# First chunk's softmax spread before normalizing, with the last down projection in 288-column pieces

## The chip, the cores and the metric

The kernel runs on one core of a Trainium2 chip. The metric is the device time of one execution in microseconds. The engines are TensorE (PE; its weight loads are shown as PEld), VectorE (DVE), ScalarE (ACT), GpSimd (POOL) and SyncE (SP), which here only issues DMAs.

## The reference

Four layers run one after the other on one sequence of 2048 rows of 576 values, all in bf16: attention, gated unit, attention, gated unit, each with a layer norm ahead and a residual sum behind. Both attention layers use the same weights, and so do both gated units.

```python
def _A_ref(x, wqkv, wo):            # H = 32 heads of Dh = 18; W, dil = 8, 2
    q, k, v = split(x @ wqkv)
    idx = pos[:, None] - arange(W)[None, :] * dil      # 8 keys, 2 rows apart, looking back
    logits = einsum("bhsd,bhswd->bhsw", q, k[idx]) * Dh ** -0.5
    logits = where(idx >= 0, logits, -1e9)
    o = einsum("bhsw,bhswd->bhsd", softmax(logits), v[idx])
    return o.reshape(B, S, D) @ wo

def _B_ref(x, w_gate, w_up, w_down):                   # F = 4608
    return ((x @ w_gate) * (x @ w_up)) @ w_down

x = x + _A_ref(_layernorm(x), A_wqkv, A_wo)
x = x + _B_ref(_layernorm(x), B_w_gate, B_w_up, B_w_down)
# the same two lines once more
```

## The kernel before

**Chunks.** The sequence is worked through in chunks of 256 rows; the first 256 rows of the first attention layer are two chunks of 128 rows. Each chunk `j` goes through `attention(j, ...)` and then `glu(j, ...)`. Eight blocks of 128 rows pass the first pair of layers, then the second pair, then the other eight blocks do the same, which makes 17 chunks.

**A planner sets the order.** Every step is an `op` with an engine, a cost in ns, keys that it reads and writes, a priority and a rank. `Plan.run` takes the steps greedily by the earliest time at which they could start by those costs, and emits the instructions in that order; each engine then works in that fixed order. A step of higher rank (a later chunk's attention) is put behind one of lower rank that is already a candidate and would be ready soon, by the tables `GUARD`, `SLACK` and `IDLE`, where `IDLE` is 2000 ns for rank 0. Where the planner sees TensorE idle in the opening, `fill` puts dummy products there (L1091), whose result nobody reads.

**The first chunk** (`j == 0`, called `fast`) runs alone in the opening:

- `head` does the layer norm: `bn_stats` (L414, L418), the inverse root by logarithm and exponential on ScalarE (L429, L430), the shift on VectorE (L434), the apply on ScalarE (L440), TensorE transposes (L456, L458) and one ScalarE copy of the transposed rows (L461).
- `project` makes queries, keys and values (L531); ScalarE and VectorE evacuate them (L613, L615, L642, L649), and ScalarE keeps the last rows for the next chunk (L660). The permuted copies of the weights (L355) are made on VectorE and ScalarE just ahead.
- Keys times queries on VectorE in four products (L686), each summed over the head's dimension by 20 small TensorE products with `Esel` (L701) into one PSUM bank. There the logits stand with head and quarter of the rows on partitions, and 8 offsets x 32 rows along the columns.
- `soft1` clamps the first 14 rows against `cap` on the first 32 partitions (L726), since those keys would lie ahead of the sequence, and takes the maximum (L727). `less` subtracts it (L731), ScalarE takes the exponential (L734), `soft2` the sum (L738), then come the reciprocal (L743) and `soft3`, the product with it (L741), whose result is `a_c`.
- `spread` copies `a_c` to all lanes of each head by TensorE products with `Bsel`, two quarters per PSUM bank (L756); ScalarE copies the first bank to `ab`, VectorE the second (L615, L613). Both use the same bank, one after the other. Of the two `boot` banks the other is held from the start for the result (`bo[1]`).
- `pv` multiplies values by these weights, one product for each of the 8 offsets (L786), in two buffers in turn, and `gather` adds them up in PSUM with an identity product: 512 columns in `bo[0]` (L790) and 128 in `bo[1]` (L791).
- ScalarE evacuates `bo[0]` and VectorE `bo[1]` to `oT` (L803, L805); `wo` is the output projection in two halves of 288 columns (L840); `res` adds the input (L810); and the next `head` follows, whose transposed rows `xnT_B` start the gated unit (L890).

**The gated unit** of a 256-row chunk uses the two halves of the array's rows at once (L914): ScalarE copies the gate (L925), VectorE multiplies it with the other product into `h` (L926). Each of three phases ends with a down projection, `down2`, of 12 blocks of 128 rows of `w_down` for each of two row blocks `i`. A product of 512 columns (L982) and one of 64 (L983) share the block of `h`; `settle2` adds the two parts to the residual on VectorE (L962). The last phase of the last chunk runs alone, with nothing behind it to overlap. Its order is written out by hand:

```python
order = [(1, x) for x in lead] + [(0, x) for x in spans(ph)] + [(1, x) for x in spans(ph)[8:]]
```

so row block 0 ends first, then row block 1. Each block's two settles write bf16 into the residual's own buffer, and one DMA of 128 x 576 on SP's queue stores it.

## Time and profile before

| | us |
|---|---|
| three runs | 1053.73, 1053.96, 1058.55 |
| median | 1053.96 |
| the profiled execution | 1053.36 |
| its span, first to last instruction | 1051.4 |

| engine | busy, us | share of the span |
|---|---|---|
| TensorE products | 1035.9 | 99% |
| TensorE weight loads | 832.5 | 79% |
| VectorE | 782.5 | 74% |
| ScalarE | 410.2 | 39% |
| GpSimd | 8.9 | 1% |

The span is counted in the trace from 0 and all places in this document are microseconds from there. The granted TensorE clock is 1.000. A duration in a row is that of one instruction, or of the stretch from the first to the last where a row stands for several (its last columns say how many). Products overlap: the distance between two starts is less than the duration of one, so both are given where it matters. Dummy products count as busy.

### The profile page before, as it was taken

How to read it: one execution, taken by the hardware profiler on the slowest of the kernel's cores; microseconds unless marked ns; L12 is line 12 of the kernel's file. 1: busy time of each engine (PE TensorE's matmuls, PEld its weight loads, DVE VectorE, ACT ScalarE, POOL GpSimd, SP SyncE). 2: the span in 40 equal slices, each digit the busy share in tenths (PEclk: the TensorE clock that was granted, in tenths of full speed). 3: DMA queues.
4: the chain of work that ended last, by engine and by line, in shares of the span. 5: the costliest groups of instructions: out<-in, count | busy, mean ns of one | idle time of the engine just before them, and what ended most of it. 6: DMA issues, size and time to landing. Idle time of an engine off the chain costs nothing.

```text
span 1051.4 us, 40011 instructions
## 1 busy us (share of the span) xinstructions
PE 1035.9 (99%) x17890; PEld 832.5 (79%) x17901; DVE 782.5 (74%) x1443; ACT 410.2 (39%) x1105; POOL 8.9 (1%) x33
## 2 busy tenths in 40 slices
PE   7999999999999999999999999999999999999998
PEld 4788788789888887778887777877887788777775
DVE  7598987988889879797979573775879748833332
ACT  6743533243434453334434233434344252232221
POOL 3000000000000000000000000000000000000000
PEclk9999999999999999999999999999999999999999
DMA  9957334442536443335352624233352334353432
GB/s 283 340 165 216 88 101 118 137 112 89 100 90 133 137 80 121 107 111 167 86 128 75 179 71 133 95 99 94 94 150 82 103 86 131 113 139 92 124 94 69
DMA packets 144252, 129.66 MB, mean 123 GB/s; under 512 B 43408, under 2 KB 143440, under 8 KB 144080
## 3 DMA queue, kind: packets, MB, share of 16 engines
q1 hardware_dynamic: 144080, 127.10, 42.6%
q8 instruction: 140, 2.29, 0.9%
q14 instruction: 32, 0.26, 0.1%
HBM read 114.02 MB, written 4.19 MB: 112 GB/s over the span
## 4 chain that ended last, share of the span: by engine, by line
PE 83%; DVE 10%; DMA 4%; ACT 1%; SPq 1%; issue 1%; DVEq 0%; ACTq 0%
PE pg L914 17%; PE pu L914 16%; PE pu L982 6%; PE acct L914 6%; PE pa L914 6%; PE pg L982 5%; PE pa L982 5%; PE acct L982 4%; PE pg L531 3%; PE pu L531 3%; DVE scr L786 2%; DVE oT L800 2%; PE pg L819 2%; DMA scr<-a_dram 1%; PE pg L942 1%; PE pu L890 1%
## 5 line engine op out<-in xcount | busy, mean ns | idle before, releaser
L914 PEld LDWEIGHTS <-wg 64*128 64x128 bf16 x4320 | 393.7, 94 | 30.8 <-issue 2.9
L914 PE MATMUL pg<-xnT_B,wg 64*128 64x256 bf16 x3200 | 412.3, 269 | 1.6 <-ACT xnT_B L461 1.1
L914 PEld LDWEIGHTS <-wu 64*128 64x128 bf16 x4320 | 392.4, 94 | 25.3 <-issue 1.7
L914 PE MATMUL pu<-xnT_B,wu 64*128 64x256 bf16 x3200 | 411.3, 269 | 1.0 <-DVE h L926 0.9
L982 PEld LDWEIGHTS <-h 64*128 64x128 bf16 x2136 | 129.1, 94 | 101.0 <-DVE h L926 0.7
L983 PE MATMUL pu<-wd,h 64*128 64x64 bf16 (+1 forms) x1020 | 192.8, 189 | 0.1
L983 PE MATMUL pg<-wd,h 64*128 64x64 bf16 (+1 forms) x1020 | 192.8, 189 | 0.0
L926 DVE TENSOR_TENSOR h<-pu,g_sb 128x512 bf16<-128x512 f32 x218 | 147.1, 686 | 49.6 <-ACT g_sb L925 48.6
L925 ACT CAST g_sb<-pg 128x512 bf16<-128x512 f32 x218 | 126.9, 586 | 105.0 <-PE pg L914 86.5
L475 ACT COPY tok<-pu 1x1 f32<-1x1 f32 x291 | 42.7, 147 | 318.9 <-PE pu L914 213.2
L914 PE MATMUL acct<-xnT_B,wg 64*128 64x256 bf16 x1120 | 152.8, 269 | 0.0
L914 PE MATMUL pa<-xnT_B,wu 64*128 64x256 bf16 x1120 | 152.4, 269 | 0.2
L982 PE MATMUL pu<-wd,h 64*128 64x512 bf16 x576 | 149.3, 377 | 0.3 <-ACT tok L475 0.3
L982 PE MATMUL pg<-wd,h 64*128 64x512 bf16 x576 | 149.1, 377 | 0.0
L983 PEld LDWEIGHTS <-h 64*128 64x128 bf16 x2136 | 127.9, 95 | 1.6 <-issue 1.1
L982 PE MATMUL pa<-wd,h 64*128 64x512 bf16 (+1 forms) x491 | 127.0, 377 | 0.0
L982 PE MATMUL acct<-wd,h 64*128 64x512 bf16 (+1 forms) x492 | 126.8, 377 | 0.0
L531 PEld LDWEIGHTS <-wqkv 64*128 64x128 bf16 (+1 forms) x2030 | 103.6, 94 | 14.5 <-issue 2.6
L707 DVE TENSOR_TENSOR scr<-qT,kv 128x1280 bf16<-128x1280 bf16 x112 | 88.5, 816 | 25.7 <-ACT kv L615 25.7
L914 PE MATMUL pg<-xnT_B,wgu_t 64*128 64x256 bf16 x400 | 107.6, 269 | 0.0
L914 PE MATMUL pu<-xnT_B,wgu_t 64*128 64x256 bf16 x400 | 107.6, 269 | 0.0
L531 PE MATMUL pg<-xnT_A,wqkv 64*128 64x256 bf16 (+2 forms) x863 | 100.5, 265 | 0.2 <-ACT wqkv L355 0.2
(156 smaller groups left out, 1488.7 us busy)
## 6 DMA issues: line engine op xcount, KB each, us to landing
wd<-in_B_w_down_dram SPq DMA_DIRECT2D x306, 288.0 KB, 4.6
scr<-a_dram SPq DMA_DIRECT2D x56, 128.0 KB, 2.7
wg<-in_B_w_gate_dram SPq DMA_DIRECT2D x6, 768.0 KB, 9.2
wu<-in_B_w_up_dram SPq DMA_DIRECT2D x6, 768.0 KB, 10.8
out_dram<-xf SPq DMA_DIRECT2D x16, 144.0 KB, 2.9
xb<-in_A_x_dram SPq DMA_DIRECT2D x7, 288.0 KB, 2.9
a_dram<-scr SPq DMA_DIRECT2D x14, 128.0 KB, 2.3
scr<-in_A_wqkv_dram SPq DMA_DIRECT2D x4, 288.0 KB, 3.5
```

Of the source, the lines that this page charges most:

```text
L475: box["at"] = nc.scalar.copy(tok[0:1, :], src())
L531: return nc.tensor.matmul(bank(p_, u)[0:m, e * n:(e + 1) * n], lhsT=wqkv[r_, k, w0:w0 + m], rhs=xnT_A[r_, k, c0:c0 + n], start=start, stop ...
L707: op("DVE", 70 + 2.6 * n, lambda p_=p_, e=e: nc.vector.tensor_tensor(late["prod"][p_ % 2][:, e, :, 0:n], qT[:, :, 0:n], kT[:, :, HALO - DI ...
L786: nc.vector.tensor_tensor(js(dst), js(vT[:, :, o0:o0 + n]), abw, op=ALU.mult)
L800: op("DVE", 70 + 2.63 * n, lambda i_=i_: nc.vector.tensor_tensor(oT[:, :, 0:n], oT[:, :, 0:n], late["prod"][i_ % 2][:, 0, :, 0:n], op=ALU. ...
L819: return nc.tensor.matmul(bank(hh, us[i])[:, 0:HD], lhsT=oT[rows, t, i * P:(i + 1) * P], rhs=wo_p[rows, t, hh * HD:(hh + 1) * HD], start=( ...
L890: nc.tensor.matmul(pt[:, e * n:(e + 1) * n], lhsT=w_[:, k, ft * P:(ft + 1) * P], rhs=xT[:, k, 0:n], start=(first and k == 0 and e == 0), s ...
L914: return nc.tensor.matmul(ps[:, e * n:(e + 1) * n], lhsT=w_, rhs=xT[rows, k, 0:n], start=(first and e == 0 and k == 0), stop=(not first an ...
L925: op("ACT", 490, lambda: nc.scalar.copy(g_sb[gs][:, 0:ul], pg[use["slot"]][:, 0:ul]), r=[f"wg_{j}_{u}"], w=[f"g{gs}"], prio=0, due=True)
L926: op("DVE", 605, lambda: nc.vector.tensor_tensor(hb[hs][:, 0:ul], pu[use["slot"]][:, 0:ul], g_sb[gs][:, 0:ul], op=ALU.mult), r=[f"wu_{j}_{ ...
L982: return [lambda: nc.tensor.matmul((pg, pu)[i][use["slot"]][:], lhsT=lhs, rhs=wt[rows, e % 2, 0:512], start=first, stop=fin, skip_group_ch ...
L983: lambda: nc.tensor.matmul((pg, pu)[i][tl["slot"]][:, 0:TL], lhsT=lhs, rhs=wt[rows, e % 2, 512:D], start=first, stop=fin, skip_group_check ...
```

## The change

The first chunk's exponentials are written as bf16 straight into `a_c` and are spread unnormalized. Sum and reciprocal run beside that; the reciprocal is split into two bf16 parts (`rz`), which eight TensorE products with `Bsel` (`sums`) spread and add up in columns 128 to 255 of `bo[1]`; ScalarE copies them to `rzs`, and the evacuation of the gathered values becomes three VectorE products with `rzs`. The output projection is cut into three steps, each of which waits for its own part of `oT`.

The mask is added instead of clamped: `cap` is now zero except for -1e9 at the masked places, and one TensorE product with the identity adds it to the logits bank of each layer's first chunk, behind the first group of logits.

The first chunk's second layer norm splits its apply, and the copy of the transposed rows, between ScalarE and VectorE. In the last down projection each product has 288 columns, half of a row; the four quarters (row block, half) end one after the other, with a settle of 128 x 288 for each into a buffer of its own (`outb`) and a DMA of its own.

```diff
     Bsel = sb("Bsel", [P, 4, 4, 32])
-    cap = sb("cap", [32, W, HALO], FP32)
+    cap = sb("cap", [P, W, HALO])
+    rz = sb("rz", [P, 2, P // 4])
+    rzs = sb("rzs", [P, P], FP32)
...
     wd = [sb(f"wd{i}", [P, 2, D]) for i in range(NWD)]
+    outb = xb[0]
...
         def mk_cap():
-            nc.gpsimd.memset(cap[:], 3e38)
+            nc.gpsimd.memset(cap[:], 0.0)
...
                 if wlist[i_] > 0:
-                    nc.gpsimd.memset(cap[:, i_, 0:DIL * wlist[i_]], -1e9)
+                    nc.gpsimd.memset(cap[0:32, i_, 0:DIL * wlist[i_]], -1e9)
...
                     nc.scalar.activation(y[:, D:D + TL], x[:, KF * P:D], ACT.Identity, **sc)
-            if "n" in parts:
+            two = halves and nst == 1
+            if two:
+                op("ACT", 490, lambda i=i: nc.scalar.activation(xn[ia + i][:, 0:320], src(i)[:, 0:320], ACT.Identity,
+                                                                bias=nmr[:, ia + i:ia + i + 1], scale=rstd[:, ia + i:ia + i + 1]),
+                   r=[keys[i], nk[i], rk[i]], w=[f"xn{ab}{ia + i}"], prio=prio)
+                op("DVE", 330, lambda i=i: nc.vector.tensor_scalar(xn[ia + i][:, 320:D], src(i)[:, 320:D], rstd[:, ia + i:ia + i + 1],
+                                                                   nmr[:, ia + i:ia + i + 1], op0=ALU.mult, op1=ALU.add),
+                   r=[keys[i], nk[i], rk[i]], w=[f"xn{ab}{ia + i}h"], prio=prio)
+            elif "n" in parts:
...
                     nc.tensor.transpose(bf(b())[r_:r_ + TL, KF, :], xn[ia + i][:, KF * P:D], ident[:])
-            o = op("PE", 290, tr, r=[f"xn{ab}{ia + i}", "ident"], prio=0, margin=mg, **b.take())
+            o = op("PE", 290, tr, r=[f"xn{ab}{ia + i}", "ident"] + [f"xn{ab}{ia + i}h"] * two, prio=0, margin=mg, **b.take())
             pl.also(o, [key + str(ia + i)])
+            if two:
+                b.use["left"] = 2
+                op("ACT", 420, lambda i=i, b=b, cs=cs: nc.scalar.copy(dst[:, 0:3, cs], bf(b())[:, 0:3]), r=[b.key], w=[key + str(ia + i)],
+                   prio=prio, **b.drop())
+                op("DVE", 330, lambda i=i, b=b, cs=cs: nc.vector.tensor_copy(dst[:, 3:KT, cs], bf(b())[:, 3:KT]), r=[b.key], w=[key + str(ia + i) + "h"],
+                   prio=prio, **b.drop())
+                continue
...
                                          stop=(i_ == len(srcs()) - 1), skip_group_check=True)
+                if t0 == 0 and p_ == 0:
+                    nc.tensor.matmul(pav[0:32, :, 0:HALO], lhsT=ident[:, 0:32], rhs=cap[:], start=False, stop=True, skip_group_check=True)
...
                 op("PE", 20 * 20, lambda p_=p_: esel(p_, lambda: [late["prod"][p_ % 2][:, :, k, :] for k in range(KT)]),
-                   r=["sel", pk], prio=0, **kw)
+                   r=["sel", pk, "cap", "ident"], prio=0, **kw)
...
             op("PE", 250 + 4 * max(45, 0.215 * n), lambda: [esel(p_, lambda p_=p_: [late["s1"][p_]]) for p_ in range(W // 2)],
-               r=["sel", "s10", "s11", "s12", "s13"], prio=0, margin=mg, **b1.take())
+               r=["sel", "s10", "s11", "s12", "s13", "cap", "ident"], prio=0, margin=mg, **b1.take())
...
             pav = wv(b1())
-            if t0 == 0:
-                nc.vector.tensor_tensor(pav[0:32, :, 0:HALO], pav[0:32, :, 0:HALO], cap[:], op=ALU.min)
...
             nc.vector.tensor_tensor(wv(late["Lt"]), pav, mx_t[:, 0:sq].unsqueeze(1).to_broadcast([P, W, sq]), op=ALU.subtract)
-        op("DVE", 130 + 2.1 * n + (250 if t0 == 0 else 0), soft1, r=[b1.key] + (["cap"] if t0 == 0 else []), w=["mx"], prio=prio - 1)
+        op("DVE", 130 + 2.1 * n, soft1, r=[b1.key], w=["mx"], prio=prio - 1)
         op("DVE", 130 + 2.1 * n, less, r=[b1.key, "mx"], w=["Lt"], prio=prio - 1, **b1.drop())
-        op("ACT", 109 + 1.66 * n, lambda: nc.scalar.activation(late["Lt"][:, 0:W * sq], late["Lt"][:, 0:W * sq], ACT.Exp),
-           r=["Lt"], w=["Lt"], prio=prio - 1)
+        ex = "a_c" if fast else "Lt"
+        op("ACT", 109 + 1.66 * n, lambda: nc.scalar.activation(late[ex][:, 0:W * sq], late["Lt"][:, 0:W * sq], ACT.Exp),
+           r=["Lt"], w=["s13" if fast else "Lt"], prio=prio - 1)
...
         def soft2():
-            nc.vector.tensor_reduce(out=zs_t[:, 0:sq], in_=wv(late["Lt"]).rearrange("p w s -> p s w"), op=ALU.add, axis=AX.X)
+            nc.vector.tensor_reduce(out=zs_t[:, 0:sq], in_=wv(late[ex]).rearrange("p w s -> p s w"), op=ALU.add, axis=AX.X)
...
             nc.vector.tensor_tensor(wv(late["a_c"]), wv(late["Lt"]), zs_t[:, 0:sq].unsqueeze(1).to_broadcast([P, W, sq]), op=ALU.mult)
-        op("DVE", 140 + 3.5 * n, soft2, r=["Lt"], w=["z"], prio=prio - 1)
+        op("DVE", 140 + 3.5 * n, soft2, r=["s13" if fast else "Lt"], w=["z"], prio=prio - 1)
         op("DVE", 300 + n, lambda: nc.vector.reciprocal(zs_t[:, 0:sq], zs_t[:, 0:sq]), r=["z"], w=["zs"], prio=prio - 1)
-        op("DVE", 86 + 2.05 * n, soft3, r=["Lt", "zs"], w=["s13"], prio=prio - 1)
+        if fast:
+            def parts_of():
+                nc.vector.tensor_copy(rz[:, 0], zs_t[:, 0:sq])
+                nc.vector.tensor_tensor(rz[:, 1], zs_t[:, 0:sq], rz[:, 0], op=ALU.subtract)
+            op("DVE", 180, parts_of, r=["zs"], w=["rz"], prio=prio - 1)
+        else:
+            op("DVE", 86 + 2.05 * n, soft3, r=["Lt", "zs"], w=["s13"], prio=prio - 1)
...
                     op("PE", 330, gather, r=["prod0", "ident"], w=[bo[0].key, bo[1].key], prio=0, hold=bo[0].pool, use=bo[0].use)
+
+                    def sums():
+                        for e in range(2):
+                            for jj in range(4):
+                                nc.tensor.matmul(bo[1]()[:, n + sq * jj:n + sq * (jj + 1)], lhsT=Bsel[:, jj].rearrange("p a b -> p (a b)"), rhs=rz[:, e],
+                                                 start=False, stop=(e == 1), skip_group_check=True)
+                    op("PE", 480, sums, r=["rz", "sel", bo[1].key], w=["rzp"], prio=0.5)
+                    op("ACT", 230, lambda: nc.scalar.copy(rzs[:], bo[1]()[:, n:2 * n]), r=["rzp"], w=["rzs"], prio=0)
...
         if fast:
-            op("ACT", 490, lambda: nc.scalar.copy(oT[:, 0:KF, 0:n], bo[0]()[:, 0:KF * n].rearrange("p (k s) -> p k s", k=KF)),
-               r=[bo[0].key], w=["oT"], prio=0, **bo[0].drop())
-            op("DVE", 200, lambda: nc.vector.tensor_copy(oT[:, KF, 0:n], bo[1]()[:, 0:n]), r=[bo[1].key], w=["oTt"], prio=0, **bo[1].drop())
+            bo[0].use["left"] = 2
+            for m in range(2):
+                op("DVE", 400, lambda m=m: nc.vector.tensor_tensor(oT[:, 2 * m:2 * m + 2, 0:n], bo[0]()[:, 2 * m * n:2 * (m + 1) * n].rearrange("p (k s) -> p k s", k=2),
+                                                                   rzs[:].unsqueeze(1).to_broadcast([P, 2, n]), op=ALU.mult),
+                   r=[bo[0].key, "rzs"], w=["oTm" if m else "oT"], prio=0, **bo[0].drop())
+            op("DVE", 200, lambda: nc.vector.tensor_tensor(oT[:, KF, 0:n], bo[1]()[:, 0:n], rzs[:], op=ALU.mult), r=[bo[1].key, "rzs"], w=["oTt"], prio=0, **bo[1].drop())
...
-                def wo(i=i, hh=hh, b=b):
-                    for t in range(KT):
+                def wo(ts, i=i, hh=hh, b=b):
+                    for t in ts:
...
-                o = op("PE", 620, wo, r=["oT", "oTt", *wok], prio=0, margin=mg, **b.take())
+                o = None
+                for ts, ky in (((0, 1), "oT"), ((2, 3), "oTm"), ((4,), "oTt")) if fast else ((range(KT), "oT"),):
+                    kw = b.take() if o is None else dict(w=[b.key], after=o)
+                    o = op("PE", 124 * len(ts), lambda ts=ts, wo=wo: wo(ts), r=[ky, *wok] + ["oTt"] * (not fast), prio=0, margin=mg, **kw)
...
         fk = [f"xf{(t0 // 2) % NXS}_{i0 + i}" for i in range(nst)]
-        xT, xk = xnT_B[j % NXB], [f"xB{j % NXB}_{i}" for i in range(nst)]
+        xT, xk = xnT_B[j % NXB], [f"xB{j % NXB}_{i}" for i in range(nst)] + ["xB0_0h"] * (j == 0)
...
                 return second
-            todo = {0: spans(ph), 1: spans(ph)}
-            lead = spans(ph)[:8]
-            order = [(1, x) for x in lead] + [(0, x) for x in spans(ph)] + [(1, x) for x in spans(ph)[8:]]
-            for x, (i, (m, e, ft)) in enumerate(order):
+            lead, rest = spans(ph)[:8], spans(ph)[8:]
+            pts = [(0, 0), (0, 1), (1, 0), (1, 1)]
+            order = [(p_, x) for p_ in pts[:3] for x in lead] + [(p_, x) for p_ in pts[:3] for x in rest] + [(pts[3], x) for x in lead + rest]
+            for x, ((i, hh), (m, e, ft)) in enumerate(order):
                 kw = dict(pair=(use, tl)) if x == 0 else {}
-                bb("PE", 122, lambda i=i, m=m, e=e, ft=ft: [f() for f in two(i, slice(0, P), m, e, ft, ft == n0, ft == n1)],
-                   r=[f"h{hsl[m]}", f"wd{wb(ft)}"], w=[f"acc{j}_{ph}{i}"], **kw)
+
+                def part(i=i, hh=hh, m=m, e=e, ft=ft):
+                    nc.tensor.matmul((pg, pu)[i][(use, tl)[hh]["slot"]][:, 0:HD], lhsT=hb[hsl[m]][:, e * n + i * P:e * n + (i + 1) * P],
+                                     rhs=wd[wb(ft)][:, e % 2, hh * HD:(hh + 1) * HD], start=ft == n0, stop=ft == n1, skip_group_check=True)
+                bb("PE", 122, part, r=[f"h{hsl[m]}", f"wd{wb(ft)}"], w=[f"acc{j}_{ph}{i}{hh}"], **kw)
                 if ft == n1:
-                    settle2(i, use, tl, True, f"acc{j}_{ph}{i}")
+                    u = (use, tl)[hh]
+                    cs = slice(hh * HD, (hh + 1) * HD)
+                    at = outb[:, i, cs]
+                    op("DVE", 370, lambda i=i, u=u, cs=cs, at=at: nc.vector.tensor_tensor(at, (pg, pu)[i][u["slot"]][:, 0:HD], xs_f[:, i0 + i, cs], op=ALU.add),
+                       r=[f"acc{j}_{ph}{i}{hh}", fk[i]], w=[f"ob{i}{hh}"], prio=0, free="unit", use=u)
+                    op("SP", 600, dma(ov[:, t0 + i, cs], at), r=[f"ob{i}{hh}"], nbytes=P * HD * 2, prio=2)
```

## The prediction

> **What bounds the kernel now.** I read the page's busy table first, then the busy time by stretches, then the order of time at both ends.
>
> ```profile
> PE 1035.9 (99%) x17890; PEld 832.5 (79%) x17901; DVE 782.5 (74%) x1443; ACT 410.2 (39%) x1105; POOL 8.9 (1%) x33
> ```
>
> TensorE is busy 99% of the span, so between the ends only less TensorE work or fewer waits can help. The stretches (microseconds, PE, PEld, DVE, ACT, POOL busy, clock, DMA) say where it is not:
>
> ```profile
> 20.00:26.00 6.00, 4.72 (x24) 2.16 (x23) 5.04 (x13) 2.14 (x6) 0.00 (x0) 1.00 1.08 328
> 34.00:60.00 26.00, 25.71 (x441) 21.72 (x441) 18.81 (x42) 15.96 (x38) 0.00 (x0) 1.00 1.05 327
> 300.00:350.00 50.00, 48.52 (x858) 42.47 (x854) 45.79 (x91) 24.28 (x67) 0.00 (x0) 1.00 0.42 99
> 600.00:1041.00 441.00, 440.99 (x7798) 350.55 (x7793) 269.02 (x485) 150.45 (x423) 0.00 (x0) 1.00 0.37 108
> ```
>
> Before 34 us TensorE waits for the first chunk and fills with dummy products (L1091), which count as busy. From 34 to 1041 us it idles 4.6 us in all (1007.0 less 1002.4 busy), most of it between 100 and 600 us, where VectorE is busy near 90%. After 1047 us only the last settles and the store remain. So the change can pay at the two ends; a microsecond of the first chunk saved moves everything behind it, as long as TensorE stays fed. The first chunk, in order of time (start, duration, engine, line):
>
> ```profile
> 16.63 0.27 DVE L726 TENSOR_TENSOR pu<-pu,cap 32x112 f32<-32x112 f32 x1
> 17.40 0.42 DVE L731 TENSOR_TENSOR scr<-pu,mx 128x256 f32<-128x256 f32 x1
> 17.92 0.42 ACT L734 ACTIVATE scr<-scr 128x256 f32<-128x256 f32 x1 [0.85 <-DVE scr L731]
> 19.37 0.42 DVE L741 TENSOR_TENSOR scr<-scr,zs 128x256 bf16<-128x256 f32 x1
> 19.85 0.38 PE L756 MATMUL pu<-scr,Bsel 128*128 128x256 bf16 x2 [0.44 <-DVE scr L741]
> 20.26 0.59 ACT L615 CAST scr<-pu 128x512 bf16<-128x512 f32 x1
> 21.37 0.69 DVE L613 CAST scr<-pu 128x512 bf16<-128x512 f32 x1 [0.53 <-DMA wgu_t<-in_B_w_up_dram]
> 22.09 3.94 DVE L786 TENSOR_TENSOR scr<-kv,scr 128x640 bf16<-128x640 bf16 x8
> 26.50 0.59 ACT L803 CAST oT<-pu 128x512 bf16<-128x512 f32 x1 [4.26 <-PE pu L790]
> 27.14 0.79 PE L840 MATMUL pg<-wo_p,oT 128*128 128x288 bf16 x5
> 27.96 0.46 DVE L810 TENSOR_TENSOR xf<-pg,xb 128x288 f32<-128x288 f32 x1
> 31.00 0.87 ACT L440 ACTIVATE xn<-xf,nmr,rstd 128x576 bf16<-128x576 f32 x1 [0.42 <-DVE nmr L434]
> 31.92 0.40 PE L456 MATMUL pg<-ident,xn 128*128 128x128 bf16 x4 [0.49 <-ACT xn L440]
> ```
>
> Each step starts within 0.1 us of the end of the one above or of an unshown one between, so this is a chain. (The wait named as a DMA at L613 is the second spread product, 20.90 to 21.28.) The other end:
>
> ```profile
> 1046.45 0.69 DVE L962 TENSOR_TENSOR xf<-acct,xf 128x512 bf16<-128x512 f32 x1 [3.66 <-PE pg L983]
> 1047.25 0.23 DVE L962 TENSOR_TENSOR xf<-pg,xf 128x64 bf16<-128x64 f32 x1
> 1047.43 0.69 DVE L962 TENSOR_TENSOR xf<-pa,xf 128x512 bf16<-128x512 f32 x1
> 1048.22 0.23 DVE L962 TENSOR_TENSOR xf<-pu,xf 128x64 bf16<-128x64 f32 x1
> ```
>
> TensorE's last product (L983, 1047.23 and 0.19) ends at 1047.42, yet VectorE ends at 1048.45.
>
> **The first chunk, step by step.** (1) The clamp L726 goes: from 16.63 to 16.94, 0.31 us. In its place one product of 112 columns adds the mask. It stands behind the first logits group, and TensorE waits 0.4 us and more for each next group, so it is hidden; uncovered it would be at most 0.22 (the 128-column gather tail L791). The mask is now filled on all partitions by POOL, before at 8.98 to 9.80 and needed at 13.48: cover 3.7 us.
>
> (2) The spread no longer waits for sum, reciprocal and product. From the exponential's end (18.34) to the spread (19.85) was 1.51; a direct hand-over is 0.06 (L741's end to L756), so 1.45 is saved and the spread starts at 19.85 - 0.31 - 1.45 = 18.09. The exponential moves to 17.61; ScalarE's permutation copy ahead of it ends at 17.06, so that holds. Sum (0.58), reciprocal (0.35) and the two small parts (0.25, between the 0.11 and 0.16 of L434 each) run on VectorE from 18.05 to about 19.35; the second spread copy needs VectorE at 19.61. Cover 0.26.
>
> (3) Spread to first value product was 2.24 (19.85 to 22.09), and its terms stay: 0.38 product, 0.59 copy, 0.38 product through the same bank, 0.69 copy, and hand-overs. But ScalarE also has the value evacuations (0.26 and 0.59) and the halo copy (0.31) near there; before, they came first. If they still do, up to 1.16 is added, and not below zero, since the terms cannot shrink. I take 0, because the first spread is ready at 18.47, before the value tails can leave TensorE, and the planner prefers a rank-0 operation due within 2 us. L786 then starts at 20.33.
>
> (4) Eight 32-column products (sums) go between the first gather and the second. At 0.055 each (16 products of L531 at 128 columns take 0.9) that is 0.44. The value products use two buffers in turn, and an even one already waits 0.2 for its gather (period 1.01 for two). The odd ones now do as well: second gather 0.3 later, and this stays to the last. The sums wait for the reciprocal's parts, ready at 19.35, long before the first gather ends at about 21.2; behind them in TensorE's queue stand the gathers alone. Bounds: 0 (sums placed later) to 0.7 (0.10 each, the weight-load row, 0.8 in all). I take +0.30. ScalarE then copies the sums (0.26) out of the bank that the gathers still fill; if the next gather must wait for that copy, 0.27 more, inside these bounds. [...] The traces here show no such pair yet.
>
> (5) The evacuation before the output projection was 0.68 (26.46 to 27.14), ScalarE beside VectorE. Now two VectorE products of 128x256 (0.42 each by L731, 0.46 from start to start) must both end before the bank is free for the projection: 0.04 + 0.46 + 0.42 + 0.04 = 0.96. The third (0.29 by L805) hides behind four projection products at 0.124. So +0.28, from 0.2 (pitch 0.41, as L786's) to 0.5 (third not hidden). The layer-norm statistics of a later chunk that stood at 26.76 to 27.82 lose their slot; they go to VectorE's 3.8 us idle before 34.77.
>
> (6) The apply splits 576 columns into 320 on ScalarE and 256 on VectorE. ScalarE's 0.87 falls by 0.22 (slope from 0.26 at 128 columns to 0.59 at 512) to 0.39 (in proportion); I take 0.30. TensorE idles 0.49 for it now. [...] The transposed copy's split (0.69) saves nothing: TensorE has the next chunk's projection until 33.8.
>
> Start: 1.76 - 0.30 - 0.28 + 0.30 = 1.48 us sooner. Weights allow it: the second weight slice lands by 28.3.
>
> **The tail.** 24 pairs of 512 and 64 columns become 48 products of 288: the same columns. The pairs run at 0.245, L840's 288-column products at 0.124, so 5.9 us either way. The order finishes three quarters early; after the last product one 128x288 settle remains (0.46, L810) in place of 0.69 and 0.23 behind a queue: 1047.42 + 0.03 + 0.46 = 1047.91 against 1048.45, 0.54 saved. The store is 72 KB, not 144 (1.8 us to landing): 0 to 0.25 less at the 330 GB/s of that burst; I take 0.10. Four stores on SP's queue (0.4 each) instead of two, three of them over 1 us earlier. Together 0.64.
>
> **The rest.** The second layer's first chunk pays the mask product on a full TensorE: 0.05 (0 to 0.22); VectorE's 0.27 there is not on the path. The planner orders everything anew; I put 0 on it, between -4.6 (all waits gone) and +4.6 (doubled).
>
> Sum: 1.48 + 0.64 - 0.05 = 2.07. The profiled run took 1053.36 (span 1051.4 and 1.96 around it), giving 1051.3; the median of the runs shown is 1053.96, 0.6 above it, so I forecast 1051.9.
>
> **Rivals.** *ScalarE's queue is next.* Value evacuations stay ahead of the first spread copy (+0.85) and sums cost 0.57: the start gives 0.36, the total 0.95, time 1053.0. For it: their order before. Against: readiness at 18.47. *The start is absorbed.* VectorE's displaced statistics delay the layer norm of the third chunk; its transposes have about 3 us in hand before the projection at 40.68. Only the tail stays: 1053.4. *Slower: VectorE's order from 100 to 600 us.* VectorE is near 90% busy and TensorE already waited 1.1, 0.9 and 0.5 there for single VectorE or ScalarE results. If a new order puts an evacuation of the gated units behind a long attention product, each such place costs 0.5 to 1.1; from three places on the gain is gone, and a doubling (+4.6) gives 1056.5. Against: the shift is nearly uniform. *Better:* the new order loses those waits: down to 1047.3.
>
> **Numbers.** 0.5% is 5.3 us, about what a measurement of this kernel can tell from no change. Forecast 0.45, ScalarE 0.22, absorbed 0.13, slower 0.11, better 0.09. All of the first three lie within 0.5%; of the slower and the better case about 0.07 each pass it, which needs seven or more lost waits, or all waits gone and more at the ends. So 0.07, 0.86, 0.07. The range, 1048.8 to 1055.6, takes in the first three with their bounds and the near halves of the other two.
>
> **What would show it.** L786's successor starts near 20.3; the gathers' period is near 1.01 with one 0.3 slip; the output projection is about 1.2 earlier, the first transposes of the gated stage near 30.4; one settle of about 0.46 ends the kernel, its end 0.5 after the last product. TensorE's idle time from 34 to 1041 us stays near 4.6. A start of the value products past 21, or idle time changed by over 2 us, would make me wrong.

## The result and the profile after

The changed kernel takes 1051.39 us (median of 22 runs, 1049.02 to 1055.67), the kernel before on the same chip 1053.53 (22 runs, 1050.99 to 1058.55). The ratio is 0.9979 with a 95% interval of 0.997 to 0.9987: some 2.2 us less, well within 0.5%. Ratios leave out two runs that were far slower than the rest, one of the kernel before (1076.78) beside the last experiments and one of x_clamp1 (3990.57). The profiled execution took 1051.13 us with a span of 1049.35 (before 1053.36 and 1051.37).

The busy line of the page, and the four stretches that were shown of before (us, then PE, PEld, DVE, ACT, POOL busy, clock, DMA share, GB/s):

```profile
PE 1033.9 (99%) x17898; PEld 827.8 (79%) x17909; DVE 783.3 (75%) x1446; ACT 409.6 (39%) x1105; POOL 8.5 (1%) x33
```

```profile
20.00:26.00 6.00, 4.78 (x34) 2.32 (x34) 4.73 (x12) 2.56 (x8) 0.00 (x0) 1.00 1.08 325
34.00:60.00 26.00, 25.70 (x442) 21.61 (x442) 19.58 (x44) 15.94 (x37) 0.00 (x0) 1.00 1.08 320
300.00:350.00 50.00, 49.43 (x874) 43.37 (x871) 45.98 (x92) 24.34 (x69) 0.00 (x0) 1.00 0.39 99
600.00:1041.00 441.00, 440.99 (x7787) 350.53 (x7784) 268.82 (x483) 151.12 (x423) 0.00 (x0) 1.00 0.37 107
```

TensorE is the bound as before. Its idle time from the first product of the gated unit to the last product is 4.73 us against 4.68, so the middle is unchanged in sum. The opening in order of time (line numbers are those of the changed kernel; L753 is the exponential, L781 the spread, L811 the value products, L826 the sums, L838 the evacuation, L417 the statistics and L443 the apply of later blocks, L437 the shift, L876 the output projection, L846 the residual, L448 the apply, L467 and L469 the transposes, L929 the gated unit):

```profile
17.61 0.42 ACT L753 ACTIVATE scr<-scr 128x256 bf16<-128x256 f32 x1 [0.57 <-DVE scr L749]
18.08 0.38 PE L781 MATMUL pu<-scr,Bsel 128*128 128x256 bf16 x2 [0.76 <-ACT scr L753]
18.55 0.59 ACT L633 CAST scr<-pu 128x512 bf16<-128x512 f32 x1 [0.33 <-PE pu L781]
19.16 0.26 ACT L633 CAST kv<-pu 64x128 bf16<-64x128 f32 x1
...
19.66 0.69 DVE L631 CAST scr<-pu 128x512 bf16<-128x512 f32 x1 [0.19 <-PE pu L781]
20.44 1.51 DVE L811 TENSOR_TENSOR scr<-kv,scr 128x640 bf16<-128x640 bf16 x3
20.98 0.38 PE L815 MATMUL pu<-scr,ident 128*128 128x512 bf16 x1 [0.56 <-DVE scr L811]
21.25 0.35 PE L826 MATMUL pg<-rz,Bsel 128*128 128x32 bf16 x8
21.46 0.38 PE L815 MATMUL pu<-scr,ident 128*128 128x512 bf16 x1
21.86 0.15 DVE L437 SCALAR_TENSOR_TENSOR nmr<-mv,rstd 128x1 f32<-128x1 f32 x1
21.92 0.27 ACT L829 COPY rzs<-pg 128x128 f32<-128x128 f32 x1 [0.92 <-PE pg L816]
...
24.54 0.38 PE L815 MATMUL pu<-scr,ident 128*128 128x512 bf16 x1
25.43 0.76 DVE L838 TENSOR_TENSOR oT<-pu,rzs 128x256 bf16<-128x256 f32 x2 [0.94 <-PE pa L469]
26.24 0.77 PE L876 MATMUL pu<-wo_p,oT 128*128 128x288 bf16 x5 [0.33 <-DVE oT L838]
26.31 0.81 DVE L417 BATCH_NORM_STATS2 st<-xb 128x6 f32<-128x288 bf16 x2
27.27 0.40 DVE L846 TENSOR_TENSOR xf<-pu,xb 128x288 f32<-128x288 f32 x1
...
29.21 0.81 DVE L417 BATCH_NORM_STATS2 st<-xf 128x6 f32<-128x288 bf16 x2
29.74 0.85 ACT L443 ACTIVATE xn<-xb,nmr,rstd 128x576 bf16<-128x576 bf16 x1
30.18 0.11 DVE L437 SCALAR_TENSOR_TENSOR nmr<-mv,rstd 128x1 f32<-128x1 f32 x1
30.49 0.64 ACT L448 ACTIVATE xn<-xf,nmr,rstd 128x320 bf16<-128x320 f32 x1
31.19 0.40 PE L467 MATMUL pu<-ident,xn 128*128 128x128 bf16 x4 [0.45 <-ACT xn L448]
31.80 0.48 ACT L474 COPY xnT_B<-pu 128x384 bf16<-128x384 bf16 x1 [0.67 <-PE pu L469]
32.31 0.29 DVE L476 COPY xnT_B<-pu 128x256 bf16<-128x256 bf16 x1 [0.61 <-ACT xnT_B L474]
```

Exponential (first row) and spread (second row) are now next to each other; in between stood sum, reciprocal and product. From the end of the last 512-column gather (L815, 24.54 + 0.38 = 24.92; its 128-column companion ends at 24.98) to L838 there is a gap that the chain of before had not. And the statistics L417 at 26.31 stand between the evacuation and the residual on VectorE. The end of the kernel:

```profile
1043.80 0.46 DVE L1058 TENSOR_TENSOR xb<-acct,xf 128x288 bf16<-128x288 f32 x1 [2.22 <-PE acct L1051]
...
1046.25 0.46 DVE L1058 TENSOR_TENSOR xb<-pu,xf 128x288 bf16<-128x288 f32 x1 [1.01 <-PE pu L1051]
```

One settle of 0.46 follows TensorE's last product (1046.21), where two and the end of a third followed before.

Since single profiles differ by a shift of the whole opening (up to 0.9 us, of a cause that was not shown; the first statistics, which wait for the first transfer, start at 2.99 in the profile of before and at 2.89 in that of after) and by waits in the middle, the experiments are read by distances inside one run. In us; a gather ends with its 512-column product, which the evacuation reads; "glu" is the first product of the gated unit:

| kernel | exponential to spread | spread to first value product | to end of last gather | to evacuation | to projection | to residual | to glu |
|---|---|---|---|---|---|---|---|
| before | 1.93 | 2.24 | 4.37 | 0.04 | 0.64 | 0.82 | 5.87 |
| after | 0.47 | 2.36 | 4.48 | 0.51 | 0.81 | 1.03 | 5.60 |
| e1_tail | 1.94 | 2.24 | 4.37 | 0.04 | 0.64 | 0.82 | 5.86 |
| e2_open | 0.47 | 2.36 | 4.48 | 0.51 | 0.81 | 1.03 | 5.60 |
| e3_norm | 1.98 | 2.50 | 4.45 | 0.04 | 0.64 | 0.82 | 5.88 |
| e4_clamp | 0.47 | 2.36 | 4.48 | 0.11 | 0.81 | 1.03 | 5.59 |
| e5_whole | 0.47 | 2.36 | 4.48 | 0.51 | 0.81 | 1.03 | 5.81 |
| e6_early_tr | 0.74 | 2.62 | 4.88 | 0.52 | 0.81 | 1.03 | 5.23 |
| e8_stats | 0.93 | 2.36 | 4.48 | 0.52 | 0.81 | 0.81 | 5.40 |
| e9_two_stores | 0.47 | 2.36 | 4.48 | 0.52 | 0.81 | 1.03 | 5.60 |
| e10_onecopy | 0.62 | 2.61 | 4.48 | 0.53 | 0.81 | 1.03 | 5.59 |
| e11_tiny | 0.47 | 2.36 | 4.48 | 0.11 | 0.82 | 1.03 | 5.59 |
| e13_clamp | 0.46 | 2.36 | 4.50 | 0.10 | 0.81 | 1.03 | 5.60 |
| x_clamp1 | 0.47 | 2.35 | 4.50 | 0.11 | 0.81 | 1.03 | 5.60 |

In e3, e6, e8 and e10 the records show a stretch of 3.4 us at half clock between 15 and 19 us (granted 0.50 from 16 to 18 us in each of the four, 1.00 in the changed kernel); that the odd figures of their first two columns (0.62 to 0.93, 2.50 to 2.62) come of it and not of the edits is the author's reading, and no run parts the two.

### The profile page after: what moved, and what is told of

It reads as the page before. It is cut to its first block, busy times and chain, and to the rows that moved or that the text cites. A ratio compares the mean times of both kernels' runs of the same rounds, so it can differ in the third digit from the quotient of the medians.

```text
span 1049.3 us, 40035 instructions
## 1 busy us (share of the span) xinstructions
PE 1033.9 (99%) x17898; PEld 827.8 (79%) x17909; DVE 783.3 (75%) x1446; ACT 409.6 (39%) x1105; POOL 8.5 (1%) x33
## 4 chain that ended last, share of the span: by engine, by line
PE 84%; DVE 10%; DMA 3%; issue 1%; ACT 1%; SPq 1%; DVEq 0%; ACTq 0%
PE pg L953 16%; PE pu L953 16%; PE pu L1021 6%; PE acct L953 6%; PE pa L953 6%; PE pa L1021 5%; PE pg L1021 5%; PE acct L1021 4%; PE pg L549 3%; PE pu L549 3%; DVE scr L811 2%; PE pg L855 2%; DVE oT L833 2%; PE pu L929 2%; PE pg L929 1%; DMA scr<-a_dram 1%
## 5 line engine op out<-in xcount | busy, mean ns | idle before, releaser
L1021 PEld LDWEIGHTS <-h 64*128 64x128 bf16 x2112 | 122.6, 94 | 102.5 <-DVE h L965 1.0
L1022 PE MATMUL pg<-wd,h 64*128 64x64 bf16 x1008 | 190.5, 189 | 0.0
L1022 PE MATMUL pu<-wd,h 64*128 64x64 bf16 x1008 | 190.5, 189 | 0.0
L1021 PE MATMUL pa<-wd,h 64*128 64x512 bf16 x480 | 123.8, 377 | 0.0
L1021 PE MATMUL acct<-wd,h 64*128 64x512 bf16 x480 | 123.7, 377 | 0.0
L1022 PEld LDWEIGHTS <-h 64*128 64x128 bf16 x2112 | 121.6, 95 | 1.2 <-issue 0.4
L549 PEld LDWEIGHTS <-wqkv 64*128 64x128 bf16 (+1 forms) x2030 | 102.8, 94 | 15.8 <-issue 3.5
L549 PE MATMUL pg<-xnT_A,wqkv 64*128 64x256 bf16 (+2 forms) x863 | 100.0, 265 | 1.1 <-DVE xf L1001 0.8
```

The lines of the kernel that those rows point to most:

```text
L549: return nc.tensor.matmul(bank(p_, u)[0:m, e * n:(e + 1) * n], lhsT=wqkv[r_, k, w0:w0 + m], rhs=xnT_A[r_, k, c0:c0 + n], start=start, stop ...
L1021: return [lambda: nc.tensor.matmul((pg, pu)[i][use["slot"]][:], lhsT=lhs, rhs=wt[rows, e % 2, 0:512], start=first, stop=fin, skip_group_ch ...
L1022: lambda: nc.tensor.matmul((pg, pu)[i][tl["slot"]][:, 0:TL], lhsT=lhs, rhs=wt[rows, e % 2, 512:D], start=first, stop=fin, skip_group_check ...
```

## The experiments

**The two ends apart.** e1_tail is the kernel before with the new last down projection (the edit shown), e2_open the changed kernel with the old one (the reverse).

```diff
-            order = [(1, x) for x in lead] + [(0, x) for x in spans(ph)] + [(1, x) for x in spans(ph)[8:]]
+            order = [(p_, x) for p_ in pts[:3] for x in lead] + [(p_, x) for p_ in pts[:3] for x in rest] + [(pts[3], x) for x in lead + rest]
...
```

> The kernel before with the new last down projection alone. Theory (the two ends add up): first value product 22.1, first gated product 33.8, last product 1047.4 as before; last settle ends 0.50 behind it (before 1.03), the store is done 2.6 behind that (before 2.9), span 1050.5. Rival (a new order of the whole moved TensorE's waits): the last product moves by 1 or more although nothing ahead of it was edited.

> The changed kernel with the old last down projection. Theory (the ends add up): first value product 20.4, first gated product 32.9, last product 1046.2, last settle 1.03 behind it, span 1050.2. Rival (order): last product away from 1046.2 by 1 or more.

Times: 1051.97 and 1057.65, one run each, beside 1052.24 of the kernel before. In e2 the last product ends at 1051.58 instead of 1046.2, by the expectation the sign of its rival. But the order of the instructions on VectorE and ScalarE is that of the changed kernel up to the last settles, so a new order is not the cause, and the time of e2 is not to be read as the opening's price: from glu to the last product it lost 5.6 us more than the changed kernel, 1.96 of it as idle time of TensorE in the unaltered middle, and a stretch of 3.4 us at half clock stands near 146 us. The rest of the loss is not explained. The distances are clean. With the old opening e1 has the opening of before to 0.01, with the new one e2 that of after. From the last product's end to the last settle's end: 0.50 in e1 and after, 1.03 in e2 and before. From there to the end of the span: 2.72 and 2.64 with the new tail, 2.92 and 3.18 with the old. The two parts do not act on each other, and the tail is worth 0.53 by the settle and 0.2 to 0.5 by the store.

**Normalizing before the spread again.** e3_norm is the changed kernel with `soft3` ahead of the spread, no sums, and the old evacuation; mask product, split apply and tail stay.

```diff
-        ex = "a_c" if fast else "Lt"
+        ex = "Lt"
...
+        op("DVE", 86 + 2.05 * n, soft3, r=["Lt", "zs"], w=["s13"], prio=prio - 1)
...
-                    op("PE", 480, sums, r=["rz", "sel", bo[1].key], w=["rzp"], prio=0.5)
-                    op("ACT", 230, lambda: nc.scalar.copy(rzs[:], bo[1]()[:, n:2 * n]), r=["rzp"], w=["rzs"], prio=0)
```

> The changed kernel with the first chunk's softmax normalized before the spread, as before, and the old plain evacuation; mask product, split layer norm and new tail stay. Theory (steps add up): first value product 21.8 (0.31 from the mask alone), first gated product 33.3, that is the spread is worth 1.35 at the value products but only 0.4 to 0.5 at the gated unit, since evacuation and displaced statistics give the rest back. Rival (the spread's saving arrives whole): first gated product 34.2.

```profile
18.24 0.42 ACT L753 ACTIVATE scr<-scr 128x256 f32<-128x256 f32 x1 [0.77 <-DVE scr L749]
...
20.22 0.38 PE L775 MATMUL pu<-scr,Bsel 128*128 128x256 bf16 x2
```

Exponential to spread is 1.98 again, against 0.47 in the changed kernel, where the exponentials are spread unnormalized and the granted clock was 1.00 in this stage. The last gather ends 4.45 behind the first value product; there are no sums in that run, but a shift (L437, 0.15) came ahead of the last value product on VectorE. Without either, before and e1 have 4.37. The changed kernel has that shift among its value products too (21.86). But its second gather starts 0.48 behind the first (20.98, 21.46), where it was 0.40 before, and ends with its 128-column product at 21.89; the fourth value product waits for that end and starts at 21.93, so that the shift need not have cost anything there. So the sums cost 0.11 at most. ScalarE's evacuation starts 0.04 behind the gather, as before.

The expected places were missed: the first value product came at 22.72 (21.8) and the first gated product at 34.55 (33.3, the rival 34.2). A later opening (0.57) and the stretch at half clock are in both. At the gated unit there is also another order on TensorE: from the first transposes to glu 2.13 us pass instead of 1.68, because 20 products of the next block's projection stand between instead of 12. So what the spread alone is worth at the gated unit, e3 does not show.

**Why the evacuation starts late.** VectorE's L838 starts 0.51 behind the last gather in the changed kernel; in the kernel before ScalarE's L803 started 0.04 behind its gather. The row names the next block's transposes (L469), which share TensorE. e6_early_tr puts these transposes between the gathers (first lines); e4_clamp has VectorE's clamp back in place of the mask product (last lines).

```diff
+            was, pl.rank = pl.rank, 0 if first_tr else pl.rank
...
+            pl.rank = was
...
+            if t0 == 0:
+                nc.vector.tensor_tensor(pav[0:32, :, 0:HALO], pav[0:32, :, 0:HALO], cap[:], op=ALU.min)
```

> The changed kernel with the second chunk's transposes (L467, L469) put between the gathers instead of behind the last one. Theory A (VectorE's evacuation waited for these transposes, as the wait view says): first evacuation product starts 0.05 behind the end of the last wide gather, 25.0 instead of 25.43, and the output projection at 25.8 instead of 26.24. Theory B (a delay of VectorE's own at this instruction): still 0.5 behind the gather, 25.4. Under both some of the second chunk's projection fills TensorE ahead of the output projection; first gated product 32.3 under A, 32.6 under B.

> The changed kernel with the clamp on VectorE in place of the mask product. Theory: maximum 0.31 later, first value product 20.75, first gated product 33.2. Rival (VectorE had slack there): first value product 20.45 and no change behind.

```profile
25.16 0.38 PE L817 MATMUL pu<-scr,ident 128*128 128x512 bf16 x1
...
26.05 0.76 DVE L840 TENSOR_TENSOR oT<-pu,rzs 128x256 bf16<-128x256 f32 x2 [0.94 <-PE pg L818]
```

This is e6 (its line numbers here are two higher). No transpose stands behind the gather, and the gap is still 0.52 (25.53 to 26.05): the transposes are not what VectorE waits for, and the name in the row was wrong. (The first gated product came at 33.12, later than either theory had it: the gathers took 0.40 longer, and TensorE waited 0.57 for the transposed copy.) In e4, where only the softmax's start was touched, the gap was 0.11. That had not been expected: the evacuation and all that it waits for were the same, and VectorE had one instruction more ahead of it. So the last runs asked what of the clamp does it. e11_tiny keeps the mask product and puts a memset of 32x8, which nobody reads, where the clamp was; e13_clamp is e4 once more, in twelve runs.

```diff
+            if t0 == 0:
+                nc.vector.memset(tiny[:], 0.0)
             nc.vector.tensor_reduce(out=mx_t[:, 0:sq], in_=pav.rearrange("p w s -> p s w"), op=ALU.max, axis=AX.X)
```

> The changed kernel with one more small VectorE instruction (a memset of 32x8) ahead of the maximum, so that every later VectorE instruction stands one place further back, as with the clamp; mask still added on TensorE, nothing else altered. Stream theory (the start of L838 0.51 us behind the last gather is tied to where VectorE's instruction stands in its stream): gap of 0.1 us or less between last gather and first evacuation product, and the output projection 0.9 us behind the gather instead of 1.3. Clamp theory (the gap goes only with what the clamp itself does, a read and write of the score bank on VectorE): the gap stays at 0.51. Chance theory (the gap comes and goes from run to run): either; then the kernel with the clamp, run again beside it, may show 0.5 as well. Time 1050 to 1053 us.

> The kernel with VectorE's clamp in place of the mask product, again, timed. If the 0.11 us gap ahead of the evacuation is a property of the program and not of one run, it is 0.11 again. Forecast from it: 0.4 us sooner at the evacuation, 0.25 to 0.31 later at the maximum, so 0 to 0.2 us sooner at the first gated product than the changed kernel: 1051.2 us, 0.998 of the time before, not to be told from the changed kernel.

```profile
16.76 0.06 DVE L747 MEMSET tiny<- 32x4 uint32 x1
...
24.72 0.38 PE L818 MATMUL pu<-scr,ident 128*128 128x512 bf16 x1
...
25.20 0.76 DVE L841 TENSOR_TENSOR oT<-pu,rzs 128x256 bf16<-128x256 f32 x2 [0.54 <-PE pg L819]
...
26.02 0.77 PE L879 MATMUL pu<-wo_p,oT 128*128 128x288 bf16 x5
```

This is e11 (line numbers three higher). The memset of 0.06 us, eight microseconds earlier, takes 0.40 us out of the evacuation's start: 0.11 behind the gather. All four kernels with one more instruction there have 0.10 or 0.11, all seven others with this evacuation 0.51 to 0.53. So it is neither the clamp nor chance, and not the transposes either, which stand behind the gather in e11 as in the changed kernel. It goes with one more instruction in VectorE's stream. But each of the four edits also changes a buffer that is declared ahead of `rzs` (`cap` in 32 bits, or `tiny`), so that later buffers may lie elsewhere; no run parts the one from the other. What in the engine does it, these runs do not show. Measured from the end of the statistics ahead of the maximum to glu, the changed kernel takes 16.21 (16.66 to 32.87), e13 16.12 (16.47 to 32.59), e11 15.82 (16.82 to 32.64): the clamp costs its 0.31 and saves 0.40 by accident, the memset saves the 0.40 alone.

As times: e13 has 1050.24 (12 runs), a ratio of 0.9967 (0.995 to 0.9984) to the kernel before on its chip; e11 1049.99 in its one run. Neither can be told from the changed kernel.

**The splits of the second layer norm.** e5_whole has apply and transposed copy whole again; e10_onecopy the copy alone, by leaving out the second `if two:` block.

```diff
-            two = halves and nst == 1
+            two = False
```

> The changed kernel with the first chunk's second layer norm whole on ScalarE: one apply, one copy of the transposed rows. Theory (the apply's split saves 0.23, the copy's split costs 0.1 since its halves run one after the other): transposes 31.4 against 31.19, their copy 0.69 long and done by about 32.7 against 32.60, first gated product 33.0 against 32.87. Rival (both splits save): first gated product 33.3 or later.

> The changed kernel with the transposed copy of the first chunk's second normalization whole again on ScalarE (the apply stays split). Bank theory (the two halves read one PSUM bank and ran one after the other, 0.80 us in all against 0.69 for the whole copy): first gated product 0.1 us sooner from the transposes on, transposes to first gated product 1.55 to 1.6 instead of 1.68. Rival (the split copy helps as planned): 0.15 us later. Time within 0.3 us of the changed kernel, 0.998 of before.

```profile
31.30 0.40 PE L467 MATMUL pu<-ident,xn 128*128 128x128 bf16 x4 [0.45 <-ACT xn L448]
...
31.91 0.69 ACT L472 COPY xnT_B<-pu 128x640 bf16<-128x640 bf16 x1 [0.67 <-PE pu L469]
...
32.98 0.62 PE L922 MATMUL pg<-xnT_B,wg 128*128 128x128 bf16 x8
```

Residual to glu is 5.81 with both whole, 5.59 with the copy whole, 5.60 with both split: the split apply is worth 0.21 in this order of TensorE's products, the split copy nothing. In the changed kernel the halves ran one after the other on their common bank, 31.80 to 32.60, in 0.80 us where the whole copy (this fence, e10) takes 0.69; but in both kernels 1.68 us pass from the first transpose to glu, because the next block's transposes stand ahead of it on TensorE (32.37 and 32.69 in the changed kernel, 32.48 and 32.80 in e10). The expectation of 0.1 us sooner failed there. e10's ratio is 0.9966 (0.9949 to 0.9982).

**The displaced statistics.** e8_stats holds the later chunks' statistics until the first chunk's second shift.

```diff
-            op("DVE", 970, stats, r=[keys[i], *xr], w=[f"mv{ab}{ia + i}", f"st{ab}{ia + i}0", f"st{ab}{ia + i}1"], prio=prio)
+            hold = late.get("nmr") if pl.rank in (3, 4) or (pl.rank == 2 and i == 1) else None
+            op("DVE", 970, stats, after=hold, r=[keys[i], *xr], w=[f"mv{ab}{ia + i}", f"st{ab}{ia + i}0", f"st{ab}{ia + i}1"], prio=prio)
...
```

> The changed kernel with the layer-norm statistics of later chunks held back until the first chunk's second shift (L437) is out. Theory (they sat in the first chunk's path three times, 0.22, 0.35 and 0.2): residual sum 27.05 instead of 27.27, shift about 29.6 instead of 30.18, transposes 30.4 instead of 31.19, first gated product 32.0 instead of 32.87, span about 1048.5. Rival (TensorE's projection for the second chunk sets the start of the gated unit): first gated product stays near 32.8. Second rival (the held-back work is late for the third chunk): a wait of TensorE near 40 us takes the gain back.

Projection to residual falls from 1.03 to 0.81, as before, and residual to glu from 5.60 to 5.40: holding the statistics back saves 0.42 of the 0.87 expected at the gated unit. Only the first 0.22 is a cost of the change. Ahead of the shift there stood statistics in the kernel before as well, and from residual to shift it had 2.89, the changed kernel 2.91:

```profile
29.93 0.77 DVE L414 BATCH_NORM_STATS2 st<-xf 128x6 f32<-128x288 bf16 x2
...
30.85 0.11 DVE L434 SCALAR_TENSOR_TENSOR nmr<-mv,rstd 128x1 f32<-128x1 f32 x1
```

But e8 is not a gain. The idle time of TensorE rises to 5.91, with new waits from 42.9 (0.49), 51.3 (0.43), 52.3 (0.79) and this one (the output projection of the third chunk, waiting for VectorE):

```profile
58.77 0.79 PE L879 MATMUL pa<-wo_p,oT 128*128 128x288 bf16 x5 [0.98 <-DVE oT L836]
```

What VectorE does not do at 26 and 29 us it does ahead of the third chunk, and TensorE waits there for 2.7 us (busy for 23.27 of the 26.00 us from 34 to 60, 25.70 in the changed kernel). Time 1052.65, one run.

**The stores.** e9_two_stores is the changed kernel with two stores of 144 KB instead of four of 72.

```diff
-                    op("SP", 600, dma(ov[:, t0 + i, cs], at), r=[f"ob{i}{hh}"], nbytes=P * HD * 2, prio=2)
+                    if hh:
+                        op("SP", 600, dma(ov[:, t0 + i, :], outb[:, i, :]), r=[f"ob{i}0", f"ob{i}1"], nbytes=P * D * 2, prio=2)
```

> The changed kernel with one store of 144 KB for each row block instead of one of 72 KB for each quarter; settles unchanged. Theory (the last store's size is worth 0.3): the span ends 2.9 behind the last settle instead of 2.6. Rival (size does not matter, the order of the stores does): 2.6.

From the last settle's end to the end of the span 3.96 (after 2.64). Of this, 1.05 is one of the sixteen landings of the last store behind the others (1050.40 against 1049.35), which no other run's last store has; the others landed 1.81 behind the issue (1047.54), as in the kernel before (1.82), against 1.59 for 72 KB. So the smaller last store is worth 0.22, by one run.

**A candidate to beat both.** x_clamp1 is the changed kernel with clamp and whole copy.

> Both together, a candidate to beat both kernels: clamp on VectorE and whole transposed copy. If both readings hold, first gated product 0.2 to 0.3 us sooner than in the changed kernel and time about 1050.9 us, 0.9975 of before; that is less than the spread of single runs (4 us), so only an interval against the kernel before can be had, and it will overlap with the changed kernel's 0.997 to 0.9987.

Ratio 0.9959 (0.9943 to 0.9976) to the kernel before, beside 0.9967 and 0.9966 of e13 and e10 on the same chip. It beats the kernel before; against the changed kernel (0.997 to 0.9987) the intervals overlap. Its profile has the 0.11 gap and the opening's distances of e13, and no more: from the statistics to glu 16.12, 0.09 less than the changed kernel, where 0.2 to 0.3 had been expected.

## Why the prediction was right, and where its terms were wrong

The forecast was 1051.9 and the median 1051.39; the sum of 2.07 us stands against 2.02 in the span. That is closer than its terms were. The start gave 0.96 us at glu instead of 1.48, the tail 0.81 instead of 0.64, and 0.25 came between. That last figure is not a result of the change: TensorE's busy time from glu to the last product (1008.91 before, 1008.61 after) lies anywhere between 1008.25 and 1009.97 in the other profiles (e2 aside). Errors cancelled: the start was 0.52 short, the tail 0.17 and the middle 0.25 more than forecast, and the 0.05 for the second layer's mask product, which no run prices, is not seen. That the sum is right to 0.05 is luck; the steps that pay, opening and tail, were right in kind. Column by column the start is 1.77 up to the spread, less 0.12 (to the value products), 0.11 (gathers), 0.64 (evacuation) and 0.21 (residual), and 0.27 more from there to glu.

- **(1) Clamp and (2) spread: right.** Spread at 18.08, forecast 18.09. e3 shows the 1.5 us and e13 the 0.31 each by itself.
- **(3) Spread to value products: right in kind.** 2.36 for 2.24. ScalarE took the first spread copy (18.55) before the value evacuations (19.16), which was the step that the first rival denied. L811 starts at 20.44, forecast 20.33.
- **(4) Sums: over-sized.** Forecast +0.30, measured +0.11 at most. The second gather does slip, by 0.08, and that stays to the last. The price of 0.055 for a product was that of 128 columns; eight products of 32 columns took 0.35 in all, 0.025 from start to start. ScalarE's copy of the sums (L829) starts at 21.92, 0.03 behind the end of the next gather into that bank (21.89), and the bank's third gather, which waits for a semaphore of that copy, comes at 22.24, 0.05 behind the copy's end. The first rival's 0.57 was the 0.30 and another 0.27 for this wait; no run shows the 0.27. The wait is there, but costs about 0.03: the 128-column product starts 0.24 behind its 512-column one, where those of the other seven gathers start 0.21 to 0.22 behind theirs. The gather's larger half goes to the other bank meanwhile (from 22.00).
- **(5) Evacuation: under-sized.** Forecast 0.96 from gather to projection, measured 1.32. The two products are 0.76 together, less than the 0.88 forecast; the miss is the start, 0.51 in place of 0.04. e6 excludes the transposes, e11 and e13 tie it to one more instruction in VectorE's stream (or to the buffers moved with it). Without it the step would have been 0.92.
- **The displaced statistics: wrong.** They were to go into VectorE's idle time before 34.77 at no cost. The block that had stood at 19.78 went to 26.31, ahead of the residual, and cost 0.21 there (0.82 to 1.03; e8 takes it back). The block at 29.21, ahead of the shift, costs 0.20 by e8, but the kernel before paid for one in that place too. The second rival (late statistics cost the third chunk) is what e8 shows where they are really put off.
- **(6) Split apply: 0.23 measured on ScalarE (0.87 to 0.64), 0.21 at glu (e5);** forecast 0.30, taken between 0.22 by the slope over the columns and 0.39 in proportion, of which the slope was the better. The split copy saves nothing, as forecast. Two things that the forecast left out stand beside it. ScalarE is still at the second chunk's apply (L443, 29.74 to 30.59) when the shift is ready, so that the first chunk's apply starts 0.31 behind the start of the shift (before 0.15), and from residual to transposes 3.92 us pass against 3.96. And from transposes to glu it is 1.68 against 1.91, because 12 products of the next block's projection stand between instead of 16. Both hold for e5 as well, with the whole apply.
- **The tail.** Settle 0.53, forecast 0.54. The store was forecast at 0.10 and gave 0.28 (2.92 to 2.64), 0.22 of it by the landing.
- **The slower rival** did not come about: the idle time of TensorE stayed. But single runs of these kernels show 3.26 to 6.69 of it, so that it is no fixed number.

## What to carry to other kernels

Work on a chain is best priced by what each removed step leaves behind on the engine's queue: here the displaced statistics took back 0.21 of 1.77 us, and pushing them out of the way made TensorE wait for 2.7 us in a later stage (e8). Where a start is late by several tenths with nothing left to wait for, move the instruction by one place in its stream before looking for a producer: here the 0.51 fell to 0.11 (e11). The name in the wait's row was no help: with the named transposes moved away the gap was still 0.52 (e6). Before a step is split between two engines, see what else stands ahead of the consumer: here the split apply gave 0.21 (e5), and the copy's halves, which read one PSUM bank in turn (0.80 against 0.69 for the whole copy), gained nothing (e10), since the next block's transposes stand ahead of the gated unit on TensorE.

## What the runs showed of the hardware

- VectorE's first evacuation product started 0.51 to 0.53 us after the end of the last gather in seven kernels (the changed one, e2, e5, e6, e8, e9, e10) and 0.10 or 0.11 in four that have one more instruction on VectorE ahead of it, be it a clamp of 0.27 us (e4, e13, x_clamp1) or a memset of 0.06 (e11). The cause is open.
- Products of 32 columns (L826) start 0.025 us apart in the changed kernel, those of 128 columns (L549) 0.056.
- ScalarE and VectorE, reading different columns of one PSUM bank (L474 and L476 of the changed kernel), ran one after the other (0.48 then 0.29, 0.80 in all); the program orders them so (L476 waits for a semaphore of L474), and whether the chip needs it was not tried.
- The last store landed 1.58 to 1.60 us after its issue with 72 KB (eleven kernels), 1.82 and 1.79 with 144 KB (the kernel before and e2). In e9, with 144 KB, fifteen of its sixteen landings came within 1.81 and one at 2.86.
- Five of the fourteen profiles hold one stretch of 3.4 us at half clock, between 15 and 19 us (e3, e6, e8, e10) or near 146 us (e2).
